# One ScalarE operation for a gated sigmoid, gate outputs sent out ahead of w_out, and weight sums made at other places

## The chip, the cores and the metric

The kernel runs on one core of one Trainium2 chip. The metric is the device time of one execution in microseconds (us).

## The reference, cut to what matters

```python
# attention: 4 batches, 12 heads, 448 rows, head size 64; w_pre and w_post are 12 x 12
scores = einsum('bhij,hg->bgij', q @ k^T / 8, w_pre)
attn = exp(scores - max); attn = attn / (sum(attn) + 1e-9)
x = (einsum('bhij,hg->bgij', attn, w_post) @ v)           # as 1792 x 768
# first layer: 768 -> 1536 -> 768
gate = 1 / (1 + exp(-(x @ w_gate)))
x = (gate * (x @ w_val)) @ w_out
# second layer: 768 -> 2048 -> 768
h = x @ w_in
out = (h * (1 / (1 + exp(-1.702 * h)))) @ w_out2
```

The weights arrive as 64-bit floating point numbers. The 1792 rows are two halves of 896 rows (t = 0 and t = 1), and each half is two groups of 448 rows.

## The kernel before, in words

**Stages.** After attention (to about 462 us) TensorE (PE) runs four stages, in the order `first(0)`, `first(1)`, `second(1)`, `second(0)`: `first(t)` is the first layer for a half, `second(t)` the second one. In `first(0)` the gate and value products go out by L875 into PSUM tiles `pg` and `pv`, and w_out's into `py`. In `first(1)` and in the first product of `second` (`inner`) the products go through `quarters` (L906 to L956), a scheme with seven products (`ORDER`) where eight are usual; their tiles are `pq`, their matmuls L922, and sums and differences of weights (L779, DVE) and of activations feed them. One call of `quarters` makes four blocks of 128 x 448 for each of two sets of weights (q = 0 and 1: gate and value in `gates`, two groups of columns in `inner`); `first(1)` calls it six times (through `gates`), and `inner` is called four times in each `second`. The last product of `second` is L1303, into `po`.

**Weights.** A unit of weights is 128 x 384 numbers. A fresh one (`ws`) is turned into 32 bits by one ScalarE (ACT) operation (`bits`, L744) and four DVE operations (L750, L756, L762, L768) on a tile `wc`, and stored in DRAM (`kept`). Each weight that PE uses is split into a high part (`high`, ACT, L805) and a low part (`low`, DVE, L811) in one of five tiles `w`; three products of high and low parts take the place of one. `split` writes out one step of this chain, `ahead` keeps the chain four or five units ahead of PE's use. A load from `kept` (`stage`, L738, issued on SP's DMA queue) waits until its tile `ws` is free, which a sum L779 can decide.

**Extra conversions.** `whole(rest.pop(0), False)` in `__init__` (L604 to L613) puts conversions of w_out2's and w_in's weights, which nobody needs yet, at chosen places of the chain.

**Sums of w_out2.** `sums_out` (L1000) makes sums of w_out2's weights for the last product and stores them in `sums2` (`sb` in the trace). For each of eight numbers kc it yields ten items: two empty ones, the load of two blocks from `kept` (L1012), two empty ones, two subtractions (`t1`, `t2`, through `tt`, L1036), then four times `put`: a cast to a high part (ACT, L903), a low part (DVE, L904), a store (L1018). `later_work(todo, hooks)` sets a rate of `len(todo) / hooks` items per hook, and `pump(ease)`, which `quarters` calls after each product with `EASE[p]` (2.0 for p = 6 and 5, 0.4 to 1.1 for the others), writes out as many items as the rate has earned. So the order of DVE's, ACT's and SP's instructions is fixed when the kernel is written out, and each engine runs its own list in order.

**Deferred work.** `after(n, f)` puts an operation on the list `later`; `ahead` ends with `flush(False)`, which writes out what is due and counts the rest down.

**Gates.** In `gates` the last group's product gets a multiply (`tt`) one hook later, and its high and low part (`hilo`, L903, L904) one hook after that; the results G are what w_out's product L875 reads.

**The activation.** In `inner`, `done` computes the sigmoid with ACT into a PSUM bank (L976) and multiplies one hook later on DVE (`tt`, L1036): 8 in a call, 64 in the eight calls of both halves, 48 of them `xy<-s,pq` and 16 `xy<-c,pq`.

Of the kernel before, what the change touches and what calls it, by code (L numbers as in the profile page):

```python
# [9 lines left out]
F32 = mybir.dt.float32  # L10
F32R = mybir.dt.float32r
U32 = mybir.dt.uint32
AF = mybir.ActivationFunctionType
ALU = mybir.AluOpType
# [508 lines left out]
class Ffn:  # L523
# [14 lines left out]
    PW = KG * 128  # L538
# [7 lines left out]
    def __init__(self, ctx, tc, xd, yd, kept, sums2, w_gate, w_val, w_out, w2_in, w2_out, out):  # L546
        self.ctx, self.tc, self.nc, self.xd, self.out, self.kept = ctx, tc, tc.nc, xd, out, kept
        self.yd, self.sums2 = yd, sums2
        self.S = xd[0].shape[2]
        self.KD = w_gate.shape[0] // 128  # L550
        self.K1 = w_gate.shape[1] // 256
        self.K2 = w2_in.shape[1] // 256
        self.NBLK = len(xd) // 2
        self.NN = w_gate.shape[0] // self.PW
        self.NT = 2 * self.S // 128
        KG, KD, K1, K2 = self.KG, self.KD, self.K1, self.K2
        self.pieces = []
        for f in range(K1):
            for w in (w_gate, w_val):
                self.pieces += [self.block(w, k0, KG, f * 128, 128) for k0 in range(0, KD, KG)]  # L560
        o1 = len(self.pieces)
        for m in range(KD):
            self.pieces += [self.block(w_out, k0, KG, m * 128, 128) for k0 in range(0, K1, KG)]
        for f in range(K2):
            self.pieces += [self.block(w2_in, k0, KG, f * 128, 128) for k0 in range(0, KD, KG)]
        o2 = len(self.pieces) - 2 * K2
        o3 = len(self.pieces)
        HK = self.HK = K2 // 2
        self.o3 = o3
        self.pieces += [self.block(w2_out, half * HK + kc, 1, n * self.PW, self.PW)  # L570
                        for kc in range(HK) for n in range(self.NN) for half in range(2)]


        self.items = []
        self.units = []
        self.used = []

        def whole(i, used=True):
            u = len(self.units)
            self.units.append(("f", len(self.items), i))  # L580
            self.items.append(("f", i, u + 1))
            if used:
                self.used.append(u)

        def kept_pair(i):
            u = len(self.units)
            self.used += [u, u + 1]
            self.units += [("p", len(self.items), x) for x in range(2)]
            self.items.append(("k", i, u + 3))

        def kept_sums(i):

            u = len(self.units)
            n = len(self.items)
            for f in range(2):
                for g in range(2):
                    self.items.append(("k", i[g][f], u + (10 + g if f == 0 else 14 + g)))
            for p in self.ORDER:
                for g in range(2):
                    self.used.append(len(self.units))  # L600
                    self.units.append(("s", n + g, p))

        rest = [*range(o3, len(self.pieces)), *range(o2, o3)]
        for i in range(o2):  # L604
            whole(i)
            if 6 <= i < o1 and (i % 3 or i in (12, 36)) or i > o1 and i % 2:
                whole(rest.pop(0), False)
        for j in range(0, K1, 2):
            kept_sums([[4 * (j + f) + 2 * g for f in range(2)] for g in range(2)])
            for _ in range(1 if j >= K1 - 6 else 0):  # L610
                whole(rest.pop(0), False)
        for i in range(o1, o2, 2):
            kept_pair(i)  # L613
            for _ in range(2):
                if rest:
                    whole(rest.pop(0), False)
        assert not rest
        self.ends = []
        for t in range(2):
            for f in range(0, K2, 4):  # L620
                kept_sums([[o2 + 2 * (f + 2 * g + x) for x in range(2)] for g in range(2)])
            self.ends.append((len(self.units) + 2, len(self.items)))
            self.units += [("x", None, None)] * 3
        self.limit, self.most = self.ends[0]
        self.want = set(self.used)
        self.ready = {}
        self.conv = {}
        self.sums = {}
        self.staged = []
        self.later = []  # L630
        self.done = set()
        self.step = 0
        self.taken = 0
        self.turn = 0
        self.blocks = deque()
        self.places = 0
        self.home = []
        self.maker = None
        self.credit = 0.0
        self.loads = None  # L640
# [331 lines left out]
    def inner(self, raw, last):  # L972

        def done(q, f, h, y, bank):
            dst = self.plain(raw[2 * q + f])[:, h * self.S:(h + 1) * self.S]
            self.after(0, lambda: self.nc.scalar.activation(bank, y, AF.Sigmoid, scale=1.702))  # L976
            self.after(1, lambda: self.tt(dst, y, bank, ALU.mult))

        self.quarters(self.A, done, last)

# [20 lines left out]
    def sums_out(self, kcs, ring=3):  # L1001


        nc, PW = self.nc, self.PW
        own = [self.form(F32) for _ in range(3)]
        x, y, t = (b[:, :, :PW] for b in own)
        outs = deque(self.form() for _ in range(ring))
        b11, b21, b12, b22, t1, t2 = x[:, 0], x[:, 1], y[:, 0], y[:, 1], t[:, 0], t[:, 1]

        def load(kc):  # L1010
            for i, d in enumerate((x, y)):
                nc.sync.dma_start(d, self.kept[self.o3 // 2 + 2 * kc + i].rearrange("a p f -> p a f"))  # L1012

        def put(kc, p, src, *after):
            outs.rotate(1)
            out = outs[0][:, :, :PW]
            self.hilo(out, src)
            self.after(1, lambda: nc.sync.dma_start(self.sums2[kc][p], out.bitcast(F32)))  # L1018
            for a in after:
                self.tt(*a, ALU.subtract)  # L1020

        for kc in kcs:
            yield lambda: None
            yield lambda: None
            yield lambda kc=kc: load(kc)
            yield lambda: None
            yield lambda: None
            yield lambda: (self.tt(t1, b12, b11, ALU.subtract), self.tt(t2, b22, t1, ALU.subtract))
            for p, src, *after in ((6, t2), (5, t1, (b11, b22, b12)), (7, b11, (t2, b21, t2)), (4, t2)):
                yield lambda kc=kc, p=p, src=src, after=after: put(kc, p, src, *after)  # L1030
        yield lambda: None
        yield lambda: None
        yield lambda: self.give(*own, *outs)
# [89 lines left out]
    def first(self, t):  # L1123

        K1, S = self.K1, self.S
        G = []
        if t:
            self.later_work(self.sums_out(range(4), 5), 55)
        for f in range(K1):
            G.append([self.form() for _ in range(2)])  # L1130
            if t and f % 2:
                self.gates(G[f - 1:], f == K1 - 1)
                if f == K1 - 5:
                    self.rush()
            elif not t:
                if f == 0:
                    pg, pv = (acc for acc, _ in self.going)
                else:
                    pg = self.banks("pg", 2)
                    self.products(pg, self.X)  # L1140
                    pv = self.banks("pv", 2)
                    self.products(pv, self.X)
                self.gated(G[f], pg, pv)
        if not t:
            self.give(*(x for c in self.X for x in c))
        self.next = {p: [] for p in self.ORDER}
        if t:
            self.A = self.next
            self.later_work(self.sums_out(range(4, 5)), 17)
        steps = K1 // self.KG  # L1150
        for m in range(self.KD):
            py = self.banks("py", 2)
# [10 lines left out]
            else:  # L1163
                for h in range(2):
                    y = self.temp("y")
# [45 lines left out]
    def second(self, t):  # L1211

        nc, S, PW, HK = self.nc, self.S, self.PW, self.HK
# [44 lines left out]
        for f in range(4):  # L1258
            raw += [self.form(F32) for _ in range(4)]
            last = f == 3  # L1260
            if f == 0 and t:
                self.later_work(self.sums_out(range(5, HK), 5), 27)
            elif f > 1:
                self.rush()
                self.later_work(work[:HK] if f == 2 else work[HK:], 12)
            if last:
                self.loads = (seq, False)
            self.inner(raw[4 * f:], last)
# [8 lines left out]
        outs = self.out[t * 2 * S:(t + 1) * 2 * S]  # L1277
# [162 lines left out]
```

## Time and profile before

| what | value |
|---|---|
| time, median of 3 runs | 1396.62 us (1396.53 to 1397.7) |
| the profiled execution, its own time | 1400.11 us |
| its span | 1398.1 us |
| mean granted clock of TensorE | 0.999 of full speed |
| instructions | 26028 |

The span is from the first to the last instruction of the profiled execution; the 2.0 us beyond it lie around the program. In rows of the trace a line such as L811 is a line of this kernel, PE is TensorE's matrix products and PEld its weight loads, DVE is VectorE, ACT is ScalarE, SPq is the queue in which SyncE issues DMAs. `w<-wt,w` reads: writes a tile w, reads tiles wt and w. What stands in square brackets is idle time ahead of the row and what ended it.

### The profile page before, as it was taken

The page shows a single profiled execution, that of the slowest core. Times are in us where ns is not written, and L with a number is a line of the kernel's source. Part 1 is how long each engine was busy: PE and PEld are TensorE (multiplying, and loading weights), DVE is VectorE, ACT ScalarE, POOL GpSimd, SP SyncE. Part 2 cuts the span into 40 slices and gives each one's busy share as a digit, 9 for nine tenths or more (in the row PEclk, how much of TensorE's full clock was granted, in tenths as well). Part 3 has the DMA queues.
Part 4 walks back from the last instruction along what each step waited for, and adds up shares of the span by engine and source line. Part 5 has one row for each costly group of instructions (what it writes and reads, how often), then busy time and mean ns, then how long its engine had stood idle before and what let it go on. Part 6 is the DMA issues. An engine that isn't in the chain of part 4 may idle for free.

```text
span 1398.1 us, 26028 instructions
## 1 busy us (share of the span) xinstructions
PE 1370.6 (98%) x8976; PEld 1247.2 (89%) x8976; DVE 1113.5 (80%) x2622; ACT 834.6 (60%) x1953; POOL 168.5 (12%) x159
## 2 busy tenths in 40 slices
PE   7999999999999999999999999999999999999998
PEld 5888888888887999999999989899889999999998
DVE  6777677867879789989989897875988679778664
ACT  6877788877879445445455555433656455566352
POOL 3444244434430000000000000000000000000000
PEclk9999999999999999999999999999999999999999
DMA  6644534622526588889884542673442587222584
GB/s 164 187 141 134 157 117 138 186 90 88 169 101 225 182 271 267 266 260 299 285 275 126 172 149 80 197 260 135 143 151 63 149 279 254 71 69 69 153 256 155
DMA packets 213699, 242.36 MB, mean 173 GB/s; under 512 B 69420, under 2 KB 201280, under 8 KB 213568
## 3 DMA queue, kind: packets, MB, share of 16 engines
q1 hardware_dynamic: 212544, 240.47, 54.3%
q8 instruction: 70, 1.15, 0.4%
q14 instruction: 61, 0.50, 0.1%
q10 hardware_dynamic: 960, 0.23, 0.1%
q0 software_dynamic: 64, 0.01, 0.0%
HBM read 149.04 MB, written 53.08 MB: 145 GB/s over the span
## 4 chain that ended last, share of the span: by engine, by line
PE 69%; DVE 16%; DMA 7%; ACT 4%; issue 3%; SPq 0%; POOL 0%; DVEq 0%; ACTq 0%; POOLq 0%
PE pq L922 21%; PE po L1303 15%; PE pso L327 9%; PE py L875 7%; PE psp L282 5%; PE psv L346 5%; PE psq L242 4%; DMA ws<-in_moe_w_out_dram 3%; DVE wc L762 3%; DVE wc L768 2%; DVE w L811 2%; DVE xy L904 2%; DVE wc L750 1%; PE pst L207 1%; ACT ex L296 1%
## 5 line engine op out<-in xcount | busy, mean ns | idle before, releaser
L922 PE MATMUL pq<-xy,w 128*128 128x448 f32 x1764 | 361.8, 366 | 4.1 <-DVE w L811 4.1
L922 PEld LDWEIGHTS pq<-xy,w 128*128 128x128 f32 x1764 | 330.3, 188 | 35.0 <-DVE w L811 7.0
L1303 PE MATMUL po<-wf,xy 128*128 128x384 f32 x1200 | 209.3, 336 | 0.0
L1303 PEld LDWEIGHTS po<-wf,xy 128*128 128x128 f32 x1200 | 209.0, 188 | 0.1
L275 POOL TENSOR_TENSOR ghl<-gt,ghl 120x448 fp32r<-120x448 f32 (+1 forms) x143 | 163.7, 1149 | 239.5 <-ACT ghl L211 180.0
L875 PE MATMUL py<-xy,w 128*128 128x448 f32 x864 | 177.5, 367 | 3.2 <-DVE xy L904 2.8
L327 PEld LDWEIGHTS pso<-w,ex 120*112 120x112 f32 (+1 forms) x1440 | 158.8, 177 | 24.5 <-issue 6.5
L875 PEld LDWEIGHTS py<-xy,w 128*128 128x128 f32 x864 | 163.0, 189 | 17.4 <-DVE xy L904 3.1
L327 PE MATMUL pso<-w,ex 120*112 120x120 f32 (+1 forms) x1440 | 171.8, 270 | 4.4 <-ACT w L309 1.6
L282 PE MATMUL psp<-ghl,wphl 120*120 120x448 f32 x540 | 139.8, 384 | 2.2 <-ACT ex L296 1.1
L289 DVE TENSOR_REDUCE st<-psp 120x1 f32<-120x448 f32 x180 | 108.8, 613 | 33.5 <-PE psp L282 32.8
L744 ACT ACTIVATE wc<-ws 128x384 f32<-128x384 f32 x136 | 75.0, 556 | 78.7 <-DMA ws<-in_moe_w_in_dram 36.4
L296 ACT ACTIVATE ex<-psp,st 120x448 f32<-120x448 f32 x180 | 113.2, 634 | 9.6 <-DVE st L289 3.6
L903 ACT CAST xy<-xy 128x384 fp32r<-128x384 f32 (+1 forms) x176 | 79.2, 473 | 47.6 <-DVE xy L1036 44.1
L282 PEld LDWEIGHTS psp<-ghl,wphl 120*120 120x120 f32 x540 | 88.8, 182 | 16.0 <-ACT ex L296 3.1
L904 DVE TENSOR_TENSOR xy<-xy 128x384 fp32r<-128x384 f32 (+1 forms) x176 | 85.1, 502 | 13.8 <-ACT xy L903 13.4
L875 PE MATMUL pg<-xy,w 128*128 128x448 f32 x432 | 91.5, 368 | 0.0
L875 PE MATMUL pv<-xy,w 128*128 128x448 f32 x432 | 91.2, 368 | 0.0
L875 PEld LDWEIGHTS pv<-xy,w 128*128 128x128 f32 x432 | 81.1, 188 | 8.2
L875 PEld LDWEIGHTS pg<-xy,w 128*128 128x128 f32 x432 | 80.9, 188 | 8.2
L211 ACT CAST ghl<-gt 120x448 fp32r<-120x448 f32 (+1 forms) x132 | 74.3, 569 | 14.5 <-PE psp L282 8.7
L805 ACT CAST w<-wc 128x384 fp32r<-128x384 f32 x72 | 36.8, 512 | 75.6 <-DVE wc L768 75.2
(92 smaller groups left out, 1980.7 us busy)
## 6 DMA issues: line engine op xcount, KB each, us to landing
gt<-sc SPq DMA_DIRECT2D x172, 210.0 KB
kept<-wc SPq DMA_DIRECT2D x136, 192.0 KB
ws<-kept SPq DMA_DIRECT2D x68, 384.0 KB
wf<-sb SPq DMA_DIRECT2D x64, 384.0 KB
ws<-in_moe_w_out_dram SPq DMA_DIRECT2D x56, 384.0 KB
ws<-in_moe_w_in_dram SPq DMA_DIRECT2D x32, 384.0 KB
sb<-xy SPq DMA_DIRECT2D x32, 384.0 KB
wf<-kept SPq DMA_DIRECT2D x64, 192.0 KB
```

Source lines behind the costliest of these rows:

```text
L211: (eng.copy if eng is nc.scalar else eng.tensor_copy)(dst, src)
L275: eng.tensor_tensor(out=t[:m, 1], in0=gt.pop(s)[:m], in1=t[:m, 0].bitcast(F32), op=ALU.subtract)
L282: nc.tensor.matmul(ps[:m, :S], wphl[:m, wp, :m], t[:m, gp], start=(i == 0), stop=(i == 2))
L289: nc.vector.tensor_reduce(out=st[:m, 0:1], in_=pre[s][:m, :S], axis=AX.X, op=ALU.max, negate=True)
L296: nc.scalar.activation(t[:m], pre.pop(s)[:m, :S], AF.Exp, bias=st[:m, 0:1], scale=1.0, accum_out=st[:m, 1:2])
L327: nc.tensor.matmul(ps[:JC, c, :, :n], e[:m, c * JC:(c + 1) * JC], w[:m, :, :n], start=True, stop=True)
L744: self.nc.scalar.activation(c.bitcast(F32), self.staged[self.units[i][1]][:, :, 1].bitcast(F32), AF.Abs)
L875: self.nc.tensor.matmul(acc[hb][:, :self.S], st, act[k0 + kc][hb][:, ap], start=(k0 + kc == 0 and part == 0 and ap == 0), stop=(k0 + kc == ...
L903: self.nc.scalar.copy(dst[:, 0], src)
L904: self.after(n, lambda: self.nc.vector.tensor_tensor(out=dst[:, 1], in0=src, in1=dst[:, 0].bitcast(F32), op=ALU.subtract))
L922: nc.tensor.matmul(x, st, A[p][c][:, ap], start=(first and c + part + ap == 0), stop=(c == self.KG - 1 and part == 1), skip_group_check=no ...
L1303: nc.tensor.matmul(acc[:, :PW], x[:, part], w[:, wp], start=(start and part == 0 and wp == 0), stop=(stop and part == 1), skip_group_check ...
```

## The change

1. In `inner`, one ACT operation (`AF.Gelu_apprx_sigmoid`) writes the activation's result directly; the sigmoid into PSUM and the DVE multiply are gone.
2. In `first`, all deferred work is written out (`self.flush()`) after the gates, before w_out's product.
3. `sums_out` is spread otherwise: kc 0 to 2 (before: 0 to 3) in the gates of `first(1)`, kc 3 (before: 4) in its w_out product, kc 4 to 7 (before: 5 to 7) in `inner` of `second(1)`, on as many hooks as before. Its `put` remembers which blocks have a store that is still to be written out, flushes if it meets one again, and with a rate over 1 flushes once at p = 7.
4. Two extra conversions move from the beginning of w_out's pieces of `first(0)` to the gates of `first(1)`, where after each `kept_sums` but the first one now stands one (before: after the last three).

```diff
@@ __init__
-            if 6 <= i < o1 and (i % 3 or i in (12, 36)) or i > o1 and i % 2:
+            if 6 <= i < o1 and (i % 3 or i in (12, 36)) or i > o1 + 4 and i % 2:
                 whole(rest.pop(0), False)
         for j in range(0, K1, 2):
             kept_sums([[4 * (j + f) + 2 * g for f in range(2)] for g in range(2)])
-            for _ in range(1 if j >= K1 - 6 else 0):
+            for _ in range(1 if j >= 2 else 0):
                 whole(rest.pop(0), False)
@@ inner
-            self.after(0, lambda: self.nc.scalar.activation(bank, y, AF.Sigmoid, scale=1.702))
-            self.after(1, lambda: self.tt(dst, y, bank, ALU.mult))
+            self.after(0, lambda: self.nc.scalar.activation(dst, y, AF.Gelu_apprx_sigmoid))
@@ sums_out
+        waiting = set()
...
             outs.rotate(1)
-            out = outs[0][:, :, :PW]
+            block = outs[0]
+            if id(block) in waiting:
+                self.flush()
+            waiting.add(id(block))
+            out = block[:, :, :PW]
             self.hilo(out, src)
-            self.after(1, lambda: nc.sync.dma_start(self.sums2[kc][p], out.bitcast(F32)))
+            self.after(1, lambda: (waiting.discard(id(block)),
+                                   nc.sync.dma_start(self.sums2[kc][p], out.bitcast(F32))))
+            if p == 7 and self.rate > 1:
+                self.flush(False)
@@ first
-            self.later_work(self.sums_out(range(4), 5), 55)
+            self.later_work(self.sums_out(range(3), 5), 55)
...
                 self.gated(G[f], pg, pv)
+        self.flush()
         if not t:
...
-            self.later_work(self.sums_out(range(4, 5)), 17)
+            self.later_work(self.sums_out(range(3, 4)), 17)
@@ second
-                self.later_work(self.sums_out(range(5, HK), 5), 27)
+                self.later_work(self.sums_out(range(4, HK), 5), 27)
```

In the changed kernel L1012 is L1013, L1018 is L1024 and L1036 is L1044. Order of DVE at the passage from the gates of `first(1)` to w_out; `xy_11187` and `xy_11188` are the two halves of the last G. Before:

```order
L1036 TENSOR_TENSOR s_11280<-s_11280,s_11263 128x448
L750 TENSOR_SCALAR wc_11476<-wc_11476 128x384
L756 TENSOR_SCALAR wc_11476<-wc_11476 128x384
L811 TENSOR_TENSOR w_11478<-ws_11409,w_11478 128x384
L750 TENSOR_SCALAR wc_11499<-wc_11499 128x384
L762 SCALAR_TENSOR_TENSOR wc_11476<-ws_11414,wc_11476 128x384
L756 TENSOR_SCALAR wc_11499<-wc_11499 128x384
L768 SCALAR_TENSOR_TENSOR wc_11476<-ws_11414,wc_11476 128x384
L811 TENSOR_TENSOR w_11503<-ws_11409,w_11503 128x384
L762 SCALAR_TENSOR_TENSOR wc_11499<-ws_11457,wc_11499 128x384
L768 SCALAR_TENSOR_TENSOR wc_11499<-ws_11457,wc_11499 128x384
L904 TENSOR_TENSOR xy_11188<-s_11280,xy_11188 128x448
```

In the changed kernel (the same two halves are `xy_11169` and `xy_11170`):

```order
L904 TENSOR_TENSOR xy_11169<-s_11330,xy_11169 128x448
L1044 TENSOR_TENSOR s_11262<-s_11262,s_11245 128x448
L904 TENSOR_TENSOR xy_11170<-s_11262,xy_11170 128x448
L750 TENSOR_SCALAR wc_11460<-wc_11460 128x384
L756 TENSOR_SCALAR wc_11460<-wc_11460 128x384
L811 TENSOR_TENSOR w_11462<-ws_11391,w_11462 128x384
L750 TENSOR_SCALAR wc_11482<-wc_11482 128x384
L762 SCALAR_TENSOR_TENSOR wc_11460<-ws_11396,wc_11460 128x384
```

The low part of the last G stood behind two extra conversions and two low parts of weights; now it follows its multiply directly.

Order of DVE in the first call of `inner` in `second(1)`; `xy_12259` to `xy_12261` are `sums_out`'s own blocks x, y and t, `w` are weight tiles for PE. Before:

```order
L779 TENSOR_TENSOR wt_12174<-ws_11945,wt_12174 128x384
L1036 TENSOR_TENSOR xy_12259<-xy_12260 128x384
L811 TENSOR_TENSOR w_12366<-wt_12350,w_12366 128x384
L779 TENSOR_TENSOR wt_12199<-ws_11999,wt_12199 128x384
L904 TENSOR_TENSOR xy_12266<-xy_12261,xy_12266 128x384
L904 TENSOR_TENSOR xy_12265<-xy_12261,xy_12265 128x384
L1036 TENSOR_TENSOR xy_12261<-xy_12259,xy_12261 128x384
L811 TENSOR_TENSOR w_12387<-wt_12174,w_12387 128x384
L904 TENSOR_TENSOR xy_12264<-xy_12259,xy_12264 128x384
L904 TENSOR_TENSOR xy_12263<-xy_12261,xy_12263 128x384
L931 TENSOR_TENSOR c_12428<-s_12426,pq_12377 128x448
L811 TENSOR_TENSOR w_12408<-wt_12199,w_12408 128x384
```

In the changed kernel (x, y and t are `xy_12241` to `xy_12243`):

```order
L904 TENSOR_TENSOR xy_12246<-xy_12241,xy_12246 128x384
L1044 TENSOR_TENSOR xy_12243<-xy_12241,xy_12243 128x384
L811 TENSOR_TENSOR w_12347<-wt_12331,w_12347 128x384
L779 TENSOR_TENSOR wt_12181<-ws_11981,wt_12181 128x384
L904 TENSOR_TENSOR xy_12245<-xy_12243,xy_12245 128x384
L811 TENSOR_TENSOR w_12374<-wt_12156,w_12374 128x384
L1044 TENSOR_TENSOR xy_12243<-xy_12242,xy_12241 128x384
L1044 TENSOR_TENSOR xy_12243<-xy_12242,xy_12243 128x384
L931 TENSOR_TENSOR c_12413<-s_12411,pq_12364 128x448
L811 TENSOR_TENSOR w_12395<-wt_12181,w_12395 128x384
L904 TENSOR_TENSOR xy_12244<-xy_12243,xy_12244 128x384
```

Before, one pair of subtractions for a new kc stands in this call (ahead of these rows); now a second one, for the next kc, stands four instructions behind the sum L779 of `wt_12181`, and `w_12395` with the add L931 behind the pair.

Order of SP's DMA queue at the same place; `kept62` to `kept65` are w_out2's blocks for `sums_out`, `kept41`, `kept42` and `kept43` are weights of w_in. Before:

```order
L738 DMA ws_12370<-kept42_103 128x2x384
L738 DMA ws_12391<-kept41_102 128x2x384
L1018 DMA sb5_6_177<-xy_12266 256x1x384
L1018 DMA sb5_5_176<-xy_12265 256x1x384
L1012 DMA xy_12259<-kept64_125 128x2x384
L1012 DMA xy_12260<-kept65_126 128x2x384
L1018 DMA sb5_7_178<-xy_12264 256x1x384
L1018 DMA sb5_4_175<-xy_12263 256x1x384
```

In the changed kernel:

```order
L738 DMA ws_12351<-kept42_103 128x2x384
L1024 DMA sb4_6_169<-xy_12248 256x1x384
L738 DMA ws_12378<-kept41_102 128x2x384
L1024 DMA sb4_5_168<-xy_12247 256x1x384
L1024 DMA sb4_7_170<-xy_12246 256x1x384
L1013 DMA xy_12241<-kept62_123 128x2x384
L1013 DMA xy_12242<-kept63_124 128x2x384
L1024 DMA sb4_4_167<-xy_12245 256x1x384
L738 DMA ws_12438<-kept43_104 128x2x384
```

The loads of `kept62` and `kept63`, which stood ahead of both loads of w_in's weights, stand behind them and behind three stores of the kc before.

## Rows read from the trace of the kernel before

**Rows 1.** The page's first part: engine, busy us (share of the span), instructions.
```profile
PE 1370.6 (98%) x8976; PEld 1247.2 (89%) x8976; DVE 1113.5 (80%) x2622; ACT 834.6 (60%) x1953; POOL 168.5 (12%) x159
```
**Rows 2.** PE's waits from 455 us on: us in total, times, longest.
```profile
PE pq L922 <- DVE w L811: 4.1, 6, 1.4
```
**Rows 3.** PE's timeline: start us, us, line, tiles, count, idle before and its end.
```profile
639.42 66.84 PE L875 MATMUL py<-xy,w 128*128 128x448 f32 x328
...
727.89 107.04 PE L922 MATMUL pq<-xy,w 128*128 128x448 f32 x524
...
835.50 2.10 PE L922 MATMUL pq<-xy,w 128*128 128x448 f32 x9 [0.57 <-DVE w L811]
...
838.30 45.84 PE L922 MATMUL pq<-xy,w 128*128 128x448 f32 x223 [0.70 <-DVE w L811]
...
883.98 13.91 PE L875 MATMUL py<-xy,w 128*128 128x448 f32 x68
...
900.65 75.47 PE L875 MATMUL py<-xy,w 128*128 128x448 f32 x364 [2.76 <-DVE xy L904]
...
975.96 29.92 PE L922 MATMUL pq<-xy,w 128*128 128x448 f32 x146
...
1025.30 9.68 PE L922 MATMUL pq<-xy,w 128*128 128x448 f32 x45 [1.42 <-DVE w L811]
...
1082.92 104.72 PE L1303 MATMUL po<-wf,xy 128*128 128x384 f32 x600
...
1187.48 102.50 PE L922 MATMUL pq<-xy,w 128*128 128x448 f32 x504
...
1289.82 104.56 PE L1303 MATMUL po<-wf,xy 128*128 128x384 f32 x600
```
**Rows 4.** Windows: stretch, us, busy of PE, PEld, DVE, ACT, POOL, PEclk, DMA, GB/s.
```profile
901.00:904.00 3.00, 3.00 (x10) 2.69 (x9) 1.24 (x4) 1.09 (x3) 0.00 (x0) 0.52 1.04 339
...
976.00:1001.00 25.00, 25.00 (x124) 23.04 (x123) 23.18 (x46) 16.00 (x34) 0.00 (x0) 1.00 0.42 139
1001.00:1027.00 26.00, 23.66 (x113) 20.77 (x113) 21.99 (x45) 14.03 (x31) 0.00 (x0) 1.00 0.48 171
```
**Rows 5.** Timeline of DVE: the low parts of the last G.
```profile
893.74 0.62 DVE L904 TENSOR_TENSOR xy<-s,xy 128x448 fp32r<-128x448 f32 x1
...
899.98 0.62 DVE L904 TENSOR_TENSOR xy<-s,xy 128x448 fp32r<-128x448 f32 x1
```
**Rows 6.** Timeline of DVE: where two extra conversions begin in the gates.
```profile
824.65 0.35 DVE L750 TENSOR_SCALAR wc<-wc 128x384 f32<-128x384 f32 x1
...
852.16 0.35 DVE L750 TENSOR_SCALAR wc<-wc 128x384 f32<-128x384 f32 x1
```
**Rows 7.** Groups by line: busy us, mean ns, idle before.
```profile
L1036 DVE TENSOR_TENSOR xy<-s,pq 128x448 f32<-128x448 f32 x48 | 29.1, 613 | 0.2
...
L976 ACT ACTIVATE pq<-s 128x448 f32<-128x448 f32 x48 | 26.4, 549 | 43.7 <-DVE s L931 43.3
...
L896 ACT ACT_TABLE_LOAD x1 | 1.3, 1283 | 0.0
```
**Rows 8.** Timeline of SP's queue and DVE in the first call of inner.
```profile
989.06 1.77 SPq L738 DMA_DIRECT2D ws<-kept  x2
...
989.85 0.55 DVE L779 TENSOR_TENSOR wt<-ws,wt 128x384 f32<-128x384 f32 x1
...
992.77 1.51 SPq L1012 DMA_DIRECT2D xy<-kept  x2
```
**Rows 9.** The chain that ended last: start us, us, DMA from issue to landing.
```profile
892.76 3.60 DMA ws<-in_moe_w_in_dram
...
996.24 6.38 DMA ws<-kept
...
1015.44 4.19 DMA xy<-kept
```
**Rows 10.** Timeline of DVE: where it waited for a load of `sums_out`.
```profile
1019.65 1.62 DVE L1036 TENSOR_TENSOR xy<-xy 128x384 f32<-128x384 f32 x3 [2.11 <-DMA xy<-kept]
```

## The prediction

> **What bounds the kernel now.** I read the page's first part, then PE's waits, its timeline stage by stage, windows around each wait, then the instruction lists of DVE and SP there. PE is busy for 98% of the span, DVE 80%, ACT 60% [rows 1]: work taken from DVE or ACT is worth nothing by itself, only where PE waited for it. After attention PE's waits are few. For low parts of weights (L811) it waited 4.1 us in six places [rows 2], two of them in the gates of the second half (0.57 and 0.70), the others in the first `inner` (the longest 1.42); 2.76 us went at one place, w_out's product of the second half, for the low part of the last G [rows 3]. The last 210 us (second `inner` and the product after it) show no wait: 1187.48 to 1289.82 is 102.34 us, which is 0.203 us for each of 504 matmuls. I use that as the clean price of a matmul and of an `inner`. The first `inner` took 1082.92 - 975.96 = 106.96, so it loses 4.6. The same w_out product took 727.89 - 639.42 = 88.47 in the first half and 975.96 - 883.98 = 91.98 in the second [rows 3].
>
> So four places can move: the gates, w_out's product behind them, the first `inner`, and the first half's w_out product.
>
> **w_out's product of the second half.** The low part of the last G's first piece ran at 893.74, that of the second at 899.98 [rows 5], with eleven list positions between. PE had reached the point where it needs it at 883.98 + 13.91 = 897.89 and went on at 900.65 [rows 3]. Now the low part stands directly behind its multiply, with only the cast on ACT between: some 2 us after 893.74, so ready near 896, ahead of 897.89. The 2.76 go. Behind that wait PE ran at half clock for a while: in the 3 us from 901 the granted clock was 0.52, that is the lower of its two levels, 1.2 GHz, and PE had stood idle just before [rows 4]. Its price: 364 matmuls at 0.203 are 74.1, the row says 75.47, so 1.3 us. Together **-4.1**. The low parts of weights behind the two pieces come up to a microsecond later, and PE reaches them 4 us sooner; in its 364 matmuls there it waited for none [rows 3], so I cost this at nothing, and at up to 1 if that lead is too short.
>
> **The gates.** One kc of sums less (eight DVE operations of about half a microsecond, 4 us), two extra conversions more, which are four DVE operations and one of ACT each. The nearest rows: the extra conversion that begins at 824.65 is followed by the two waits (1.27 together), the next, at 852.16, by none [rows 3, 6]. Two more cost 0 to 2.5 by that; the sums that leave speak for the lower half. A gain of 1.27 is the bound below, should the thinner sums clear the old waits. I take **+1.0**. The first half's w_out product loses the two conversions; its one wait there is below 0.5, so I put 0 to -0.5 and take **0**.
>
> **The activation.** 64 multiplies of 613 ns go from DVE, and the activation's 549 ns on ACT stay [rows 7]. In the second `inner` PE doesn't wait, so half of them are worth nothing. In the first `inner` eight go per call, 8 x 0.55 = 4.4 us of DVE in 26 us; this is the only place where they can matter. A table load comes in for the new function (1283 ns in the one row there is [rows 7]); ACT is busy for 16 of the 25 us from 976 [rows 4], so I cost it at nothing; without that cover it would be 1.3.
>
> **The first `inner`: sums at a higher rate.** This term decides the sign. Four kc instead of three on 27 hooks are 43 / 27 = 1.59 items per hook instead of 33 / 27 = 1.22, and EASE doubles it for p = 6 and 5. Between the load of a kc and its subtractions stand three items, so at 3.2 items a hook the subtractions are written out one hook after the load: one hook is 9 matmuls, 1.83 us, while a load takes 4.19 from issue to landing [rows 9]. DVE runs its list in order, and behind the pair of subtractions stand the add L931 and the low part of the twelfth weight tile.
>
> When does the load start? SP issues in order too. Ahead of it now stand the load of `kept41`, which needs the sum L779 of the tile it replaces, and two stores. Before, L779 ran at 989.85 and ended at 990.40 [rows 8]. In the changed list it loses two multiplies ahead of it (-1.1) and gains three low parts and a subtraction (+1.9), so it ends at about 991.4. From there SP needs what it needed before: from L779's end to the second of the two loads 0.5 for the waiting one, 1.2 for the two stores and 0.76 (half of 1.51 [rows 8]), which is 993.9. Landing takes 3.60 to 6.38 in rows of equal or similar loads; 4.19 is the one of this very kind [rows 9]: **998.0**. DVE reaches the pair at 992.4 (L779's end and two operations) and idles 5.6. Then six operations of some 0.55 (two subtractions, the cast, the copy L927 behind it on ACT, L931, L811) are 3.3 us: the tile is there at 1001.3. PE wants it when eleven tiles of 9 matmuls are done: 975.96 + 99 x 0.205 (29.92 / 146 [rows 3]) = 996.3. **PE stands 5.0 us**, against none in this stretch before, and then runs slow for 1.3, as behind the 2.76.
>
> In the second call the pattern comes again, with three DVE operations instead of four between the sum and the pair. The kernel before has a mild form of it: DVE waited 2.11 us for such a load at 1019.65 [rows 10], and PE 0.36 and 1.42 behind it. I take 3.5, between that 1.8 and the first one's 5.0, and 1.3 for the clock. The other calls have credit to spare once the eight multiplies of each are gone: 0. So the first `inner` loses 5.0 + 3.5 + 2 x 1.3 = 11.1 instead of 4.6: **+6.5**. Bounds: 2 (only the short waits stay) and 15.5 (landing 6.38 twice) of loss, so -2.6 to +10.9.
>
> The Trainium skill, "DMA: Bandwidth & Descriptors", section "Rules for kernel authors", says to issue a transfer early and to wait on it late. By that rule this part of the change goes the wrong way, and the row of 4.19 against a hook of 1.83 agrees.
>
> **Sum.** -4.1 + 1.0 + 0 + 6.5 = +3.4. The profiled execution's own time was 1400.11 us (span 1398.1), which would become 1403.5; it lies 3.5 above the median of the runs, 1396.62, so for the median **1400.0 us**, slower by 0.24%. About 0.2% (2.8 us) is what a measurement of this kernel can tell from no change: faster is below 1393.8, slower above 1399.4.
>
> **Rivals.**
>
> *The freed DVE wins (faster).* The 4.4 us per call bring every low part early, and loads land in time. Then the first `inner` loses nothing: -4.1 + 1.0 - 4.6 = -7.7, **1388.9**. For it: all waits of that stage were on DVE's low parts, and DVE was busy for 23.18 of 25 us there [rows 4]. Against it: in the first call this is only decided if the second load starts by 996.3 - 3.3 - 4.19 = 988.8, five microseconds ahead of my 993.9; SP would have to get past `kept41` without the wait for L779. Chance 0.24, with what lies up to 1393.8.
>
> *Stalls, but shorter.* The loads land in 3.60 [rows 9], so PE stands 4.4 and 2.9, and the clock doesn't fall: behind the wait of 1.42 it stayed at 1.00 [rows 4]. 7.3 - 4.6 = +2.7, with -3.1 from the rest -0.4: **1396.2**, no change. Against it: the only row behind a wait over 2 us shows the fall. Chance 0.28.
> For the landing time the Trainium skill, "DMA: Bandwidth & Descriptors", section "Anatomy of one DMA", which fits transfers that GpSimd issues, gives a fixed 2.0 us and bytes over 436 GB/s: an estimate of 2.9 us for 384 KB. By that each stall would be 1.3 shorter than in my sum and the time 1397.4, within no change; the loads of this trace are all slower, so I give this little of that chance.
>
> *The change doesn't do what it says*: the new function could reload its table in alternation with the copies and casts around it, 1.3 each time on ACT. The instruction list of the changed kernel has one load more and no others, so I give this no chance of its own.
>
> **How the numbers follow.** Forecast 0.48 (1399.4 to 1405), shorter stalls 0.28 (1393.8 to 1399.4), freed DVE 0.24 (1386 to 1393.8): these are also the chances of slower, same and faster. The range from 1389.5 to 1404.5 leaves out a tenth at each end: below, the freed DVE together with clear gates; above, slow landings in both stalls. The forecast's own range is 1399.4 to 1405.
>
> **What would show it right or wrong.** Right: PE goes through 897.89 without a wait and w_out's product takes about 88; in the first call of `inner` DVE has one idle stretch of some 5 us ahead of a subtraction pair (L1044), released by a load of `xy<-kept`, and PE one wait of some 5 us on L811 about 20 us into the stage, with a granted clock near 0.5 behind it; the first `inner` takes 112 to 114; the gates up to 1 us more than 156.1; the last two stages as before. Wrong: if DVE passes that pair without idle time or the first `inner` takes about 102 to 104, the forecast's main term has failed and the time is below 1393. If the wait in w_out's product is still there, the first term has.

## The result, and the profile after

The changed kernel takes 1407.07 us (median of 7 runs, 1404.38 to 1412.18) against 1397.63 us for the kernel before on the same chips (7 runs, 1396.53 to 1403.64). The ratio is 1.0071, with a 95% interval from 1.0048 to 1.0094: it is slower by 0.7%, some 9 us. The side was forecast; the size was not, and 1407.07 lies above the range (1389.5 to 1404.5). The profiled execution took 1411.32 us, its span is 1409.4.

PE's timeline from the gates of the second half on (start us, us, count, idle before and what ended it) answers to [rows 3]:

```profile
729.33 53.80 PE L922 MATMUL pq<-xy,w 128*128 128x448 f32 x263
783.74 52.51 PE L922 MATMUL pq<-xy,w 128*128 128x448 f32 x252 [0.61 <-DVE w L811]
836.49 4.15 PE L922 MATMUL pq<-xy,w 128*128 128x448 f32 x18 [0.24 <-DVE w L811]
841.36 45.84 PE L922 MATMUL pq<-xy,w 128*128 128x448 f32 x223 [0.72 <-DVE w L811]
887.04 87.56 PE L875 MATMUL py<-xy,w 128*128 128x448 f32 x432
974.43 20.75 PE L922 MATMUL pq<-xy,w 128*128 128x448 f32 x101
1001.76 26.54 PE L922 MATMUL pq<-xy,w 128*128 128x448 f32 x117 [6.58 <-DVE w L811]
1034.03 60.38 PE L922 MATMUL pq<-xy,w 128*128 128x448 f32 x286 [5.73 <-DVE w L811]
1094.25 104.72 PE L1312 MATMUL po<-wf,xy 128*128 128x384 f32 x600
1198.81 102.50 PE L922 MATMUL pq<-xy,w 128*128 128x448 f32 x504
1301.15 104.56 PE L1312 MATMUL po<-wf,xy 128*128 128x384 f32 x600
```

From one stage's start to the next one's, beside [rows 3]: gates 887.04 - 729.33 = 157.71 (before 156.09), w_out 974.43 - 887.04 = 87.39 (91.98), first `inner` 1094.25 - 974.43 = 119.82 (106.96), second `inner` 102.34 and the products behind both 104.56 (the same). The differences are +1.6 - 4.6 + 12.9 = +9.9. With the 1.4 by which the gates start later in this execution (729.33 against 727.89) that is all of the 11.3 between the spans. So the loss sits in one stage, in two waits and the slow stretches behind them, and the 2.76 us in front of the last G are gone.

The first of the two waits, on DVE (its list in order; the idle time is released by the load):

```profile
989.34 0.55 DVE L779 TENSOR_TENSOR wt<-ws,wt 128x384 f32<-128x384 f32 x1
989.81 0.56 DVE L904 TENSOR_TENSOR xy<-xy 128x384 fp32r<-128x384 f32 x1
990.28 0.56 DVE L811 TENSOR_TENSOR w<-wt,w 128x384 fp32r<-128x384 f32 x1
998.45 1.15 DVE L1044 TENSOR_TENSOR xy<-xy 128x384 f32<-128x384 f32 x2 [7.62 <-DMA xy<-kept]
1000.62 0.62 DVE L931 TENSOR_TENSOR c<-s,pq 128x448 f32<-128x448 f32 x1 [1.01 <-ACT s L927]
1001.15 0.55 DVE L811 TENSOR_TENSOR w<-wt,w 128x384 fp32r<-128x384 f32 x1
```

SP's queue at the same time, the same instructions as in the order shown above:

```profile
989.92 0.36 SPq L738 DMA_DIRECT2D ws<-kept  x1
990.38 1.18 SPq L1024 DMA_DIRECT2D sb<-xy  x2
991.65 1.69 SPq L1013 DMA_DIRECT2D xy<-kept  x2
993.39 0.53 SPq L1024 DMA_DIRECT2D sb<-xy  x1
```

And the loads in the chain that ended last (issue to landing):

```profile
992.38 5.97 DMA xy<-kept
...
1012.25 4.13 DMA xy<-kept
...
1026.12 6.21 DMA xy<-kept
```

This is the forecast's chain link by link: L779 ends, SP gets past the load of w_in's weights, two stores and two loads go out, DVE stands before the pair of subtractions, and PE's next weight tile is behind them. The load went out when I had it: the stage began 1.53 us earlier than before, and 992.38 is 17.95 us into it, where 993.9 was 17.94. But it took 5.97 us and not 4.19, and these 1.8 us account for the first wait, 6.58 where 5.0 was forecast. Windows around the two waits (us, PE, PEld, DVE, ACT, POOL, PEclk, DMA share, GB/s):

```profile
1001.76:1004.00 2.24, 2.24 (x6) 2.02 (x7) 2.17 (x5) 1.96 (x6) 0.00 (x0) 0.50 0.00 0
1004.00:1008.00 4.00, 4.00 (x14) 3.57 (x14) 3.86 (x9) 2.77 (x7) 0.00 (x0) 0.62 0.74 243
1008.00:1014.00 6.00, 6.00 (x31) 5.53 (x30) 5.00 (x10) 3.58 (x8) 0.00 (x0) 1.00 0.78 252
...
1028.30:1034.03 5.73, 0.00 (x2) 0.00 (x1) 1.64 (x4) 0.49 (x2) 0.00 (x0) 0.73 0.83 278
1034.00:1037.00 3.00, 2.97 (x8) 2.67 (x9) 3.00 (x7) 1.94 (x6) 0.00 (x0) 0.50 0.30 106
```

The fifth line lies in the second wait. Behind each wait PE runs at the lower clock level (0.50 is 1.2 GHz). 117 matmuls at 0.203 are 23.8 us and took from 1001.76 to 1028.30, 26.5; the 286 behind the second wait are 58.1 and took 60.2. So 2.8 and 2.1 us more are lost behind the 6.6 and 5.7.

### The profile page after: what moved, and what is told of

Its sections match the earlier page's. It is cut to its first block, busy times and chain, and to the rows that moved or that the text cites. A ratio compares the mean times of both kernels' runs of the same rounds, so it can differ in the third digit from the quotient of the medians.

```text
span 1409.4 us, 25998 instructions
## 1 busy us (share of the span) xinstructions
PE 1371.8 (97%) x8976; PEld 1249.1 (89%) x8976; DVE 1083.1 (77%) x2558; ACT 837.1 (59%) x1954; POOL 168.2 (12%) x159
## 4 chain that ended last, share of the span: by engine, by line
PE 66%; DVE 16%; DMA 9%; ACT 5%; issue 3%; SPq 1%; POOL 0%; DVEq 0%; ACTq 0%; POOLq 0%
PE pq L922 19%; PE po L1312 15%; PE pso L327 9%; PE py L875 8%; PE psv L346 5%; PE psp L282 5%; PE psq L242 4%; DMA ws<-in_moe_w_out_dram 3%; DVE wc L762 2%; DVE w L811 2%; DVE wc L768 2%; DVE xy L904 2%; DMA xy<-kept 2%; DMA gt<-sc 1%; DVE wc L750 1%
## 5 line engine op out<-in xcount | busy, mean ns | idle before, releaser
L922 PE MATMUL pq<-xy,w 128*128 128x448 f32 x1764 | 366.4, 369 | 14.0 <-DVE w L811 13.9
```

Source lines behind the costliest of these rows:

```text
L922: nc.tensor.matmul(x, st, A[p][c][:, ap], start=(first and c + part + ap == 0), stop=(c == self.KG - 1 and part == 1), skip_group_check=no ...
```

## The experiments

Each run's stage times are read as above; ratios are against the kernel before. The four parts of the change and the late loads were taken apart.

**The sums spread as before.** The changed kernel with

```diff
-            self.later_work(self.sums_out(range(3), 5), 55)
+            self.later_work(self.sums_out(range(4), 5), 55)
-            self.later_work(self.sums_out(range(3, 4)), 17)
+            self.later_work(self.sums_out(range(4, 5)), 17)
-                self.later_work(self.sums_out(range(4, HK), 5), 27)
+                self.later_work(self.sums_out(range(5, HK), 5), 27)
```

> The changed kernel with the sums of w_out2 spread as before: kc 0 to 3 in the gates, 4 in w_out, 5 to 7 in the first inner (33 items on 27 hooks). Theory (a new kc's load reaches its subtractions too late at the higher rate): the two long waits of PE, 6.6 and 5.7 us, go, and the clock's fall behind them; the first inner takes 102.5 to 106 instead of 119.8, gates about 2 more than 157.7, total 1390 to 1394. Rival (the higher rate is not it; a flush at p = 7 or the activation without its multiply brings the waits): a wait over 3 us stays, the first inner takes over 110, total 1400 or more.

1391.06 us, ratio 0.9957 (0.9945 to 0.997). The first `inner` takes 104.46, with one wait of 1.40; gates 157.33, w_out 87.39:

```profile
969.31 46.46 PE L922 MATMUL pq<-xy,w 128*128 128x448 f32 x227
1017.17 56.76 PE L922 MATMUL pq<-xy,w 128*128 128x448 f32 x277 [1.40 <-DVE w L811]
```

So the move of one kc into the first `inner` costs 16 us and is the whole loss; the rest of the change is a gain of 0.4%. The gates didn't get longer by the kc that came back (157.33 against 157.71), where I had expected 2.

**Loads one kc earlier.** The rate stays at 1.59; the loads of `sums_out` get a second pair of blocks.

```diff
-        own = [self.form(F32) for _ in range(3)]
+        own = [self.form(F32) for _ in range(5 if deep else 3)]
...
-            yield lambda kc=kc: load(kc)
+            yield lambda ahead=ahead: [load(k) for k in ahead]
...
-                self.later_work(self.sums_out(range(4, HK), 5), 27)
+                self.later_work(self.sums_out(range(4, HK), 5, True), 27)
```

`ahead` is the next kc (for the first kc, both).

> The changed kernel with kc 4 to 7 still in the first inner at the same rate, but with two pairs of blocks for the loads, so that each kc's load goes out one kc earlier. Theory (load to use is too short): no wait of PE over 1.5 us, first inner 102.5 to 106, total 1389 to 1394. Rival (eight operations of DVE for each kc at the higher rate are too much there): waits of PE on low parts stay, spread over the calls, first inner 110 or more, total over 1398.

1391.81 us, ratio 0.9953 (0.9938 to 0.9968). The first `inner` takes 103.57, and PE's row for it has no wait in it:

```profile
967.48 103.72 PE L922 MATMUL pq<-xy,w 128*128 128x448 f32 x504
1071.05 104.73 PE L1322 MATMUL po<-wf,xy 128*128 128x384 f32 x600
```

All four kc are made there, and DVE waits for no load. The place was not too full, the load was too late.

**The loads on another queue.** To part the wait on SP from the transfer:

```diff
-                nc.sync.dma_start(d, self.kept[...])
+                (nc.gpsimd if self.rate > 1 else nc.sync).dma_start(d, self.kept[...])
```

> The changed kernel with the loads of the sums in the first inner issued by GpSimd instead of SP, so that no load of w_in's weights that waits for its tile stands ahead of them; blocks and rate stay. If waiting behind such a load on SP is what makes them late, they go out some 2.5 us earlier, and the two waits shrink from 6.6 and 5.7 to about 4 and 3, total 1400 to 1403. If the blocks come free too late (one pair of blocks) and the landing of 6 us decides, the waits stay within 1 us of what they were, total 1406 to 1409.

1404.57 us, ratio 1.0049 (1.0033 to 1.0066); first `inner` 116.54. PE's waits and DVE's at the first pair:

```profile
996.70 25.48 PE L922 MATMUL pq<-xy,w 128*128 128x448 f32 x117 [4.75 <-DVE w L811]
1025.62 2.62 PE L922 MATMUL pq<-xy,w 128*128 128x448 f32 x9 [3.43 <-DVE w L811]
...
1028.96 58.95 PE L922 MATMUL pq<-xy,w 128*128 128x448 f32 x277 [0.72 <-DVE w L811]
```
```profile
993.40 1.15 DVE L1044 TENSOR_TENSOR xy<-xy 128x384 f32<-128x384 f32 x2 [5.80 <-DMA xy<-kept]
```

Between the two theories: GpSimd issued the first load at 986.26, 15.06 us into the stage, where SP did so at 17.22 (991.65 - 974.43). So SP's queue was worth 2.2 us for this load, and DVE's idle time fell by 1.8, from 7.62 to 5.80. Most of the wait is not SP's: the blocks come free only when the kc before has been used, and the transfer takes its time.

**The stores behind the loads.**

```diff
-            self.after(1, lambda: (waiting.discard(id(block)),
+            self.after(3 if self.rate > 1 else 1, lambda: (waiting.discard(id(block)),
...
-                self.later_work(self.sums_out(range(4, HK), 5), 27)
+                self.later_work(self.sums_out(range(4, HK), 7), 27)
```

> The changed kernel, but in the first inner each store of a sum goes out two hooks later (with seven blocks in the ring instead of five), so that the loads of the second and fourth kc stand ahead of the three stores that stood ahead of them on SP. If the 6 us from issue to landing come from these stores' traffic on the same DMA engines, landing falls to about 4.2, the loads also go out about 1.2 earlier, and PE's two waits fall from 6.6 and 5.7 to about 3.5 and 3, total 1398 to 1402. If the landing is long whatever is queued, only the 1.2 are saved: waits about 5.4 and 4.5, total 1403 to 1406.

1404.52 us, ratio 1.005 (1.0036 to 1.0063); first `inner` 118.04. The first wait falls to 4.21, the second is 6.17, longer than before. The loads:

```profile
986.18 5.06 DMA xy<-kept
...
1017.86 6.91 DMA xy<-kept
```

The total is the second theory's, but neither theory's waits came. A store that is issued right behind a load can slow it too: against the run without any stores (below), the first landing is 0.3 us longer and the second 1.3. In the 6.18 us of the second wait the DMA engines are busy for 0.93 at 309 GB/s.

**No stores there.**

```diff
+            to = [] if self.rate > 1 else [kc, kc + 4]
-                                   nc.sync.dma_start(self.sums2[kc][p], out.bitcast(F32))))
+                                   [nc.sync.dma_start(self.sums2[k][p], out.bitcast(F32)) for k in to]))
```

> The changed kernel without the 16 stores of sums in the first inner; kc 4 to 7 are instead filled in the gates and in w_out with what belongs to kc 0 to 3 (so the last product reads other sums), which puts 16 stores more there. If the load's 6 us are the stores' share of the DMA engines, ahead of it or behind it, landing falls to 3.6 to 4.5, and PE's two waits to 2 to 4 us; the first inner takes 108 to 113 instead of 119.8. If one pair of blocks and the distance decide and landing stays near 6, the first inner stays above 115. The total is not comparable, since gates and w_out carry more.

1404.39 us, ratio 1.0042 (1.0028 to 1.0057), with gates of 162.40 that carry the extra stores. The first `inner` takes 114.58, the waits are 3.88 and 3.12, the loads

```profile
989.29 4.75 DMA xy<-kept
...
1018.89 5.60 DMA xy<-kept
```

and PE's rows behind the two waits

```profile
997.44 25.71 PE L922 MATMUL pq<-xy,w 128*128 128x448 f32 x117 [3.88 <-DVE w L811]
1026.26 61.29 PE L922 MATMUL pq<-xy,w 128*128 128x448 f32 x286 [3.12 <-DVE w L811]
```

Without the stores each landing is 1.2 and 0.6 us shorter and the loads go out sooner, but two waits over 3 us remain, and 12 us of loss against 102.34. That lies between the two expectations. So the stores carry a part of the landing time; the loads of w_in's weights that go out beside them were not taken away, and how much of the rest is theirs stays open.

**No flush at p = 7.** The two lines `if p == 7 and self.rate > 1: self.flush(False)` are left out; where three sums fall on one hook the low part of the p = 6 sum is then taken after `t2` has been changed.

> The changed kernel without the flush at p = 7. If the waits come from the loads alone, this flush has little part in them: both long waits stay within 1.5 us, total 1404 to 1410. If the flush brings DVE's and SP's work into a worse order, they shrink by over 2 us each, total under 1402.

1406.26 us, ratio 1.0054 (1.0038 to 1.0071); waits 6.34 and 5.50, first `inner` 119.36. The flush has no part in the loss. The load's row is worth a look:

```profile
985.61 7.55 DMA xy<-kept
```

It went out 16.10 us into the stage instead of 17.95, and landed at 23.65 instead of 23.92: the 1.85 us of lead were lost again in a longer landing, in which the DMA engines were busy for 0.96 at 324 GB/s.

**Sigmoid and multiply as before**, in the changed kernel:

```diff
-            self.after(0, lambda: self.nc.scalar.activation(dst, y, AF.Gelu_apprx_sigmoid))
+            self.after(0, lambda: self.nc.scalar.activation(bank, y, AF.Sigmoid, scale=1.702))
+            self.after(1, lambda: self.tt(dst, y, bank, ALU.mult))
```

> The changed kernel with the sigmoid and DVE's multiply as before. Theory (the late loads set the waits): the eight multiplies of a call fall mostly into DVE's idle time ahead of the subtractions, the two long waits change by less than 2 us each, first inner 119 to 124, total 1406 to 1411, and second(0) as before. Rival (DVE's time sets that stage): 4.4 us more in each of the first calls, first inner 128 or more, total over 1413.

1414.87 us, ratio 1.0125 (1.0105 to 1.0144); waits 8.74 and 6.77 and four short ones, first `inner` 126.15. The first expectation missed: the multiplies do not fall into DVE's idle time. The second one's total was met, but not its first `inner` of 128 or more. Of the 6.3 us by which the stage grew, 3.2 are the two long waits (2.2 and 1.0) and 2.1 the short ones. Two multiplies stand ahead of the operations that free the blocks, so the first late load goes out 1.1 us later in the stage (990.39 - 971.35 = 19.04 against 17.95), and it takes 7.05 us to land and not 5.97.

**The same, with the loads one kc earlier:**

> The changed kernel with two pairs of blocks for the loads (loads one kc earlier) but with the sigmoid and DVE's multiply as before. If loads alone set the waits of the first inner, it stays at 103 to 105 and the total near 1392. If DVE's work counts as soon as the loads are early, eight multiplies a call are 4.4 us of DVE in 26 us where four kc leave little room: first inner 108 to 114, total 1396 to 1402.

1399.03 us, ratio 0.9997 (0.9981 to 1.0013); first `inner` 109.09, with waits of 1.38, 0.89 and 1.13 and two of 0.5 or less. With the loads early, the stage's multiplies (eight in each of four calls) cost 109.09 - 103.57 = 5.5 us together: now DVE's time counts.

**Two parts alone, and together.** The kernel before with the flush after the gates:

```diff
                 self.gated(G[f], pg, pv)
+        self.flush()
```

> The kernel before with the flush after the gates alone. The forecast's first term by itself: no wait in w_out's product of the second half, which takes 87.4 instead of 92.0, all else as before; total 1393 to 1394. If the wait turns into another one behind it, w_out's product takes over 90 and the total stays above 1395.5.

1394.81 us, ratio 0.9977 (0.9958 to 0.9996). w_out's product takes 87.40 and has no wait; the first `inner` takes 107.93, 1.0 more than in the profile of the kernel before. The total is 0.8 above what I expected.

The kernel before with the one activation operation:

> The kernel before with the single activation operation alone. At the old rate of the sums the 64 multiplies matter only where PE waited in the first inner: the 4.6 us lost there fall to 1 to 3, the second inner stays at 102.3, total 1394 to 1396.5, and the wait of 2.8 us in w_out's product stays. If the freed time of DVE is worth nothing there, the total stays within 1 us of before.

1395.56 us, ratio 0.9975 (0.9958 to 0.9993). The first `inner` takes 102.85 and has no wait, where I expected 1 to 3 of loss to stay, so all but 0.5 of its 4.6 us were DVE's multiplies:

```profile
901.96 73.91 PE L875 MATMUL py<-xy,w 128*128 128x448 f32 x364 [2.70 <-DVE xy L904]
975.70 103.01 PE L922 MATMUL pq<-xy,w 128*128 128x448 f32 x504
1078.55 104.92 PE L1302 MATMUL po<-wf,xy 128*128 128x384 f32 x600
```

Both in one kernel:

> The kernel before with two parts of the change, the flush after the gates and the single activation operation; sums and extra conversions as before. If the two add up: gates 155.8, w_out's product 87.4, first inner 102.9 (as each showed alone), total 1390 to 1392, below every other version but the next. If they don't, w_out's product or the first inner gets a wait of over 2 us and the total stays above 1393.

1390.79 us, ratio 0.9945 (0.9932 to 0.9959): w_out 87.39, first `inner` 102.89. They add up, to about 16 us below the changed kernel. It is the lowest median of all versions tried, but the old spread (1391.06), the early loads (1391.81) and the next one are not told apart from it.

The same with the two extra conversions moved:

> The same, and the two extra conversions moved from the first half's w_out product to the gates, as in the change: the first half's w_out product loses its waits and takes 87.4 instead of 88.5 to 90, the gates take 157.2 instead of 155.8, so the total is within 1.5 us of the run before it: 1389.5 to 1391.5. If four kc in the gates and five conversions are too much for DVE there, the gates take over 159 and the total is 1392 or more.

1391.35 us, ratio 0.9953 (0.9936 to 0.9969). The first half's w_out product takes 87.40 instead of 89.84, the gates 157.82 instead of 155.99: what one stage gains the other gives back.

## Why the prediction was right or wrong

- **The last G: right.** -4.1 was forecast; the stage fell by 4.6, and the flush alone gives it. A part of the difference is a slip in my sum: 364 x 0.203 is 73.9 and not 74.1, which makes the slow stretch 1.6 and not 1.3.
- **The gates: right.** +1.0 forecast, +1.6 measured, from the conversions rather than the sums. The counterpart was mis-sized: I put 0 for the first half's w_out product, where the two runs that differ in it alone show -2.4. In the changed kernel's own profile that stage has 88.59 against 88.47, so it doesn't appear there; in the eight variants of it above it has 87.4. Over both stages the moved conversions are worth nothing that was measured.
- **The activation: right in the place, short in the price.** I saw it only as room for the first `inner`; alone it takes 4.1 of the 4.6 us lost there. (Eight multiplies are 4.9 us by the 613 ns of [rows 7]; I had counted 0.55 each.)
- **The first `inner`: the mechanism was right, three sizes were off.** The step that failed is "I take 3.5" for the second wait together with 4.19 for the landing and 1.3 for the clock. Landing was 5.97 and 6.21, near the upper row of [rows 9] (6.38). The row of 4.19 was of a load with less traffic around it. Windows over the three landings, the first in the kernel before (columns as above):

```profile
1015.44:1019.63 4.19, 4.19 (x22) 3.83 (x21) 2.10 (x5) 0.80 (x2) 0.00 (x0) 1.00 1.01 330
...
992.38:998.35 5.97, 2.80 (x14) 2.25 (x12) 0.00 (x0) 0.00 (x0) 0.00 (x0) 1.00 1.01 333
...
1026.12:1032.33 6.21, 2.18 (x11) 1.67 (x9) 0.00 (x0) 0.00 (x0) 0.00 (x0) 0.89 1.00 336
```

  The DMA engines were busy throughout and moved 330 to 336 GB/s in each; what differs is how much they moved until the load was there: 1.38 MB, 1.99 MB and 2.09 MB. So the longer landing goes with other transfers in the way; that the stores are some of them is shown by the run without them, which others is open. The waits came to 6.6 and 5.7 (12.3) where 8.5 was forecast, and the clock to 2.8 and 2.1 (4.9) where 2.6 was. The first wait's excess is the landing's; the second's 3.5 was set between two numbers and not worked out. (A slip of 0.2 in the end of L779, which is 991.2 by my own terms, is too small to matter.) The stage's loss was 17.5 us where 11.1 was forecast and 15.5 bounded. I had held both upper ends unlikely at once; both loads were in traffic of this size, and they came together.
- **The rivals.** "The freed DVE wins" gave 1388.9, and fell on its deciding point: the load started 17.95 us into the stage, where it had to start by 12.8 (988.8). With the loads moved forward by a kc, DVE waits for none, and with the old spread no second pair stands in the first call; 1391.81 and 1391.06 result, 2 to 3 above its number. "Stalls, but shorter" needed landings of 3.60 and no fall of the clock; neither came.
- The shorter landing that the Trainium skill's page "DMA: Bandwidth & Descriptors", section "Anatomy of one DMA", gives (2.9 as an estimate) was shown by none of these loads; even without the stores the first took 4.75.
- **Issue early, wait late**, the rule that the Trainium skill gives on the same page, "DMA: Bandwidth & Descriptors", section "Rules for kernel authors": the trace agrees, and the run with early loads shows its worth here, 119.82 - 103.57 = 16.2 us of one stage.

## What to carry to other kernels

Work that is written into an engine's list at a higher rate brings its loads closer to their use; count the distance from load to use in time (here one hook, 1.83 us, against a landing of 4 to 7) before moving it, and give it another pair of blocks if it is short. Price a load by the rows of loads in similar traffic, not by one of its own kind that had less in its way. A wait of PE of several microseconds cost another one to three behind it at the lower clock in these runs, so two late loads cost more than their idle time.

## What the runs showed of the hardware that I had not expected

- The fall of the granted clock is not tied to the length of a wait alone. Behind 2.76 us of idle time it fell to 0.52 [rows 4]; behind 2.70 us at the same place in the run with the activation alone it stayed at 1.00:

```profile
902.00:905.00 3.00, 3.00 (x15) 2.79 (x16) 1.03 (x4) 0.62 (x2) 0.00 (x0) 1.00 0.97 310
```

- Where it fell, the price doesn't follow the length of the wait: 2.8 us behind 6.58 and 2.1 behind 5.73 in the changed kernel, but 3.1 behind 3.12 in the run without stores, where 286 matmuls (58.1 at 0.203) took from 1026.26 to 1087.39 and began so:

```profile
1026.26:1029.00 2.74, 2.74 (x7) 2.48 (x8) 2.74 (x6) 1.79 (x5) 0.00 (x0) 0.50 0.00 0
```
- The one operation for the whole activation is hardly longer than the sigmoid alone, 582 ns against 549 [rows 7], and one table load of 1283 ns serves all of them:

```profile
L976 ACT ACTIVATE xy<-s 128x448 f32<-128x448 f32 x48 | 27.9, 582 | 34.4 <-DVE s L931 34.4
...
L976 ACT ACT_TABLE_LOAD x1 | 1.3, 1283 | 0.0
```
